# Linear attention with a swish feed-forward: kv products on two column tiles, and a reordered first chunk

## The chip, the cores and the metric

The kernel runs on one core of one Trainium2 chip. The metric is the device time of one execution in microseconds (us). A profile is one execution; its span is about 1.8 us shorter than its time in the tables.

Engines: PE is TensorE's matmul and PEld its weight load, DVE is VectorE, ACT is ScalarE, POOL is GpSimd, SP starts most DMAs.

## The reference, cut to what matters

```python
q, k, v: (8, 8, 576, 64)                       # batch, heads, tokens, head dim
q_s = softmax(q, over head dim); k_s = softmax(k, over tokens)
kv  = einsum('bhsd,bhse->bhde', k_s, v)        # one 64x64 matrix per head
x   = einsum('bhsd,bhde->bhse', q_s, kv)       # heads side by side: (4608, 512)
h   = x @ w_in                                 # (4608, 2048)
out = (h * sigmoid(beta * h)) @ w_out          # (4608, 512)
```

The two products with w_in and w_out are nearly all of the work. The kernel handles 9 chunks of 512 tokens (the first 512 tokens of each batch, and one chunk with the 64 last tokens of all batches). While chunk n runs, side work prepares the attention of a later chunk.

## The kernel before

A chunk has 16 *units* j. Unit j is one `mm_a` (h: four matmuls of 512 columns, then a tanh on ACT and a gate on DVE) and one `mm_b` (four matmuls into the output accumulators, from the gate of unit j - 2). The parts that the change touches, with cuts marked:

```python
FIX, LASTMAIN, COLT = False, True, False
...
def kv_mm(b, jj, n=2, tag="att"):              # n pairs of heads
    t = ps.tile([P, n, 2 * D1], F32, ...)      # D1 = 65: 64 columns of v, and one for the sum
    for jl in range(n):
        j = n * jj + jl
        if b < NW: ...                         # batches 0 and 1 have another layout
        if COLT: ...                           # written, but off: see the change
        for i in range(R):                     # a pair of heads at once: 128x128 by 128x130
            nc.tensor.matmul(t[:, jl, :], ek[b][:, i, 2*j:2*j+2, :]..., va[b][:, i, 2*j:2*j+2, :]..., ...)
        nc.tensor.matmul(t[:, jl, :], ekt[...][:, ds(j * P, P)], vt[...]..., ...)   # the 64 last tokens
...
pool_cast(("in", 3), ("out", 3))               # POOL casts the last block of w_in to bf16
...
for u in range(4, NJ):                         # chunk 0, units 4 to 15
    if not (FIX and u == 5):
        mm_a(0, u)
    if FIX and u == 4:
        mm_a(0, 5)
        mm_b(0, 2)
        continue
    if FIX and u in (12, 14):                  # transposes of batch 1's q on PE
        for j in (u - 12, u - 11):
            q_pet(1, j, nc.scalar if u == 12 else nc.vector)
    mm_b(0, u - LAG)                           # LAG = 2
    if u in (9, 10): q_exp(1, u - 9)           # ACT
    if u in (9, 11): q_sum(1, (u - 9) // 2)    # DVE
    if u in (10, 12): q_mul(1, (u - 10) // 2)  # DVE: the softmax multiply
    if not FIX and u in (11, 13):
        for j in (u - 11, u - 10):
            q_pet(1, j, nc.scalar if u == 11 else nc.vector)
    if u >= 12: kz_exp(1, u - 12)              # ACT: exponentials of batch 1's k
    ...
def side(n, u):                                # chunks 1 to 8
    ...
    if u in (8 + o, 10 + o) and kb < B:        # kv in two groups of two pairs
        kv_mm(kb, (u - 8 - o) // 2)
        kv_norm(kb, (u - 8 - o) // 2)
    if 11 <= u < 15:                           # x: one matmul of 512 columns per pair
        x_mm(qc, u - 11, ...)
```

The softmax here doesn't subtract the row's maximum and nothing guards it: scores larger than these inputs give would overflow.

Of the kernel before, what the change touches and what calls it, by code (L numbers as in the profile page):

```python
# [9 lines left out]
BF16 = mybir.dt.bfloat16  # L10
F32 = mybir.dt.float32
# [6 lines left out]
def kernel(  # L18
# [10 lines left out]
    nc = tc.nc  # L29
    P = nc.NUM_PARTITIONS  # L30
    B, H, S, D = q.shape
# [5 lines left out]
    HP = H // 2  # L37
    R = 4
    MAIN = R * P
    TAIL = S - MAIN  # L40
    RW = 2 * S // P
    NW = 2
    D1 = D + 1
    LAG = 2
    FIX, LASTMAIN, COLT = False, True, False
    NCH = B + 1
    order = list(range(NCH))
    if LASTMAIN:
# [6 lines left out]
    ps = ctx.enter_context(tc.tile_pool(name="ps", bufs=1, space=bass.MemoryType.PSUM))  # L55
# [7 lines left out]
    kvp = const.tile([P, B, HP, P], BF16, name="kvp")  # L63
# [5 lines left out]
    def x_of(c):  # L69
        return xT[2] if c == B else xT[c % 2]  # L70
# [6 lines left out]
    ek, eq, rq, qsT = {}, {}, {}, {}  # L77
# [63 lines left out]
    def evac(eng, dst, src):  # L141
        if eng is nc.scalar:
            eng.copy(dst, src)
        else:
            eng.tensor_copy(dst, src)  # L145
# [18 lines left out]
    def k_exp(b, s, n=2):  # L164
        if s == 0:
            ek_buf(b)
        m = H // n
        h = slice(s * m, (s + 1) * m)
        nc.scalar.activation(
            ek[b][:, :, h, :].rearrange("p i h d -> p h i d"),  # L170
            k_st[b][:, h, 0 : R * D].rearrange("p h (i d) -> p h i d", i=R),
            ACTF.Exp,
        )

    def ktail_exp(b):
        e = slice((b % 2) * TAIL, (b % 2 + 1) * TAIL)
        nc.scalar.activation(
            ekt[(b // 2) % 2][e].rearrange("p (h d) -> p h d", h=H),
            k_st[b][e, :, R * D : R * D + D],
            ACTF.Exp,  # L180
        )

    def v_buf(b):
        t = work.tile([P, HP * RW * D1], BF16, tag="va", bufs=2, name=f"va{b}")
        if b < NW:
            va[b] = t[:].rearrange("p (j i x) -> p j i x", j=HP, i=RW)
        else:
            va[b] = t[:, 0 : R * H * D1].rearrange("p (i h x) -> p i h x", i=R, h=H)
        nc.gpsimd.memset(va[b][:, :, :, D:D1], 2.0)
# [8 lines left out]
    def v_cast(b, eng):  # L198
        evac(
            eng,  # L200
            va[b][:, :, :, 0:D].rearrange("p i h d -> p h i d"),
            v_st[b][:, :, 0 : R * D].rearrange("p h (i d) -> p h i d", i=R),
        )

    def vtail_cast(b, eng):
        e = b % 2
        rr = slice(e * TAIL, (e + 1) * TAIL)
        eng.tensor_copy(vt[(b // 2) % 2][rr, e, :, 0:D], v_st[b][rr, :, R * D : R * D + D])

    def q_exp(b, s, n=2):  # L210
        if s == 0:
            eq[b] = work.tile([P, R, H, D], BF16, tag="eq", bufs=2, name=f"eq{b}")
        m = H // n
        nc.scalar.activation(  # L214
            eq[b][:, :, s * m : (s + 1) * m, :].rearrange("p i h d -> p h i d"),
            q_st[b][:, s * m : (s + 1) * m, :].rearrange("p h (i d) -> p h i d", i=R),
            ACTF.Exp,
        )

    def q_sum(b, s, n=2):  # L220
        if s == 0:
            rq[b] = work.tile([P, 2, R, H], F32, tag="rq", bufs=2, name=f"rq{b}")
        m = H // n
        h = slice(s * m, (s + 1) * m)
        nc.vector.tensor_reduce(rq[b][:, 0, :, h], eq[b][:, :, h, :], axis=AX.X, op=ALU.add)  # L225
        nc.vector.reciprocal(rq[b][:, 1, :, h], rq[b][:, 0, :, h])

    def q_mul(b, s, n=2):
        m = H // n
        h = slice(s * m, (s + 1) * m)  # L230
        nc.vector.tensor_tensor(  # L231
            eq[b][:, :, h, :],
            eq[b][:, :, h, :],
            rq[b][:, 1, :, h].unsqueeze(3).to_broadcast((P, R, m, D)),
            ALU.mult,
        )

    def q_xbar(b):
        qsT[b] = work.tile([P, R, HP, P], BF16, tag="qsT", bufs=2, name=f"qsT{b}")
        nc.sync.dma_start_transpose(  # L240
            qsT[b][:].rearrange("p i j r -> p (i j) r"),
            eq[b][:].rearrange("p i h d -> p (i h d)"),
        )
# [11 lines left out]
        evac(eng, qsT[b][:, :, j, :], t[:])  # L255

    def kv_mm(b, jj, n=2, tag="att"):
        t = ps.tile([P, n, 2 * D1], F32, tag=tag, bufs=2 if tag == "att" else 1, name=f"kv{b}_{jj}")
        att_of[b, jj] = t
        for jl in range(n):  # L260
            j = n * jj + jl
            if b < NW:
                for i in range(RW):
                    nc.tensor.matmul(
                        t[:, jl, 0:D1],
                        ek[b][:, j, i, :],
                        va[b][:, j, i, :],
                        start=(i == 0),
                        stop=(i == RW - 1),
                    )  # L270
                continue
            if COLT:
                for i in range(R + 1):
                    for e in range(2):
                        hd = 2 * j + e
                        nc.tensor.matmul(
                            t[e * D : (e + 1) * D, jl, 0:D1],
                            ek[b][:, i, hd, :] if i < R else ekt[(b // 2) % 2][:, ds(hd * D, D)],
                            va[b][:, i, hd, :] if i < R else vt[(b // 2) % 2][:, b % 2, hd, :],
                            start=(i == 0),  # L280
                            stop=(i == R),
                            tile_position=(0, e * D),
                        )
                continue
            for i in range(R):
                nc.tensor.matmul(
                    t[:, jl, :],
                    ek[b][:, i, 2 * j : 2 * j + 2, :].rearrange("p h d -> p (h d)"),
                    va[b][:, i, 2 * j : 2 * j + 2, :].rearrange("p h d -> p (h d)"),
                    start=(i == 0),  # L290
                    stop=False,
                )
            nc.tensor.matmul(
                t[:, jl, :],
                ekt[(b // 2) % 2][:, ds(j * P, P)],
                vt[(b // 2) % 2][:, b % 2, 2 * j : 2 * j + 2, :].rearrange("p h d -> p (h d)"),
                start=False,
                stop=True,
            )

    def kv_norm(b, jj, n=2):
        t = att_of.pop((b, jj))
        rk = work.tile([P, n, 1], F32, tag="rk", bufs=2, name=f"rk{b}_{jj}")
        nc.vector.reciprocal(rk[:], t[:, :, D : D + 1])
        for e in range(2):
            r = slice(e * D, (e + 1) * D)
            dst = kvp[r, b, n * jj : n * jj + n, e * D : (e + 1) * D]
            src = t[r, :, 0:D] if b < NW or COLT else t[r, :, e * D1 : e * D1 + D]
            nc.vector.tensor_tensor(dst, src, rk[r].to_broadcast((D, n, D)), ALU.mult)  # L309

    def x_mm(c, j, eng, tag="att"):
        t = ps.tile([P, MAIN], F32, tag=tag, bufs=2, name=f"x{c}_{j}")
        if c < B:
            nc.tensor.matmul(t[:], kvp[:, c, j, :], qsT[c][:, :, j, :])  # L314
        else:
            for b in range(B):
                i, e = divmod(b, 2)
                nc.tensor.matmul(
                    t[:, ds(b * TAIL, TAIL)],
                    kvp[:, b, j, :],  # L320
                    qsT[B][:, i, j, ds(e * TAIL, TAIL)],
                )
        evac(eng, x_of(c)[:, j, :], t[:])

    h_of = {}

# [261 lines left out]
    def side(n, u):  # L588
        if n + 1 >= NCH:
            return  # L590
        qc = order[n + 1]
        kb = n + 1
        o = 2 if n == 1 else 0
        if u in (2 + o, 3 + o):
            q_exp(qc, u - 2 - o)
            q_sum(qc, u - 2 - o)
        if u in (4 + o, 5 + o):
            q_mul(qc, u - 4 - o)
            if kb < B:
                k_exp(kb, u - 4 - o)  # L600
        if u == 4 + o and kb < B:
            v_buf(kb)
            v_cast(kb, nc.gpsimd)
            vtail_cast(kb, nc.gpsimd)
        if u == 6 + o:
            if kb < B:
                ktail_exp(kb)
            q_xbar(qc)
        if u in (8 + o, 10 + o) and kb < B:
            kv_mm(kb, (u - 8 - o) // 2)  # L610
            kv_norm(kb, (u - 8 - o) // 2)
        if 11 <= u < 15:
            j = u - 11
            x_mm(qc, j, nc.scalar if j % 2 == 0 else nc.vector)
        if u == 9 and n + 2 < NCH:
            load_next(n + 2)
# [3 lines left out]
    for n in range(1, NCH):  # L620
        c = order[n]
# [47 lines left out]
```

## Time and profile before

| | before |
|---|---|
| time, median of 3 runs | 291.29 us (291.06 to 291.44) |
| span of the profiled run (time 292.26 us, above these three) | 290.5 us |
| PE busy | 278.6 us, 96% |
| chunks 2 to 5, each | 29.78 to 29.79 us |
| kv of one batch on PE | 1.14 us |

From the page of the kernel before: the span, the busy times and the chain of work that ended last.

```profile
span 290.5 us, 3880 instructions
...
PE 278.6 (96%) x1447; PEld 131.0 (45%) x1475; DVE 185.2 (64%) x299; ACT 163.9 (56%) x238; POOL 41.5 (14%) x55
...
PE 87%; DMA 4%; DVE 3%; ACT 1%; issue 1%; another core or an unknown queue 1%; SPq 0%; POOL 0%; ACTq 0%
```

PE is busy for 96% of the span and makes 87% of the chain: PE bounds this kernel. The windows view cuts the run into stretches. The first row below runs from unit 6 of chunk 0 to the first x matmul of batch 1 (I call this the *late stage* of chunk 0); the second is one chunk of the steady part.

```profile
core 0: us, PE busy (x) PEld busy (x) DVE busy (x) ACT busy (x) POOL busy (x), PEclk, DMA share, GB/s
26.40:49.69 23.29, 21.63 (x140) 10.72 (x142) 16.46 (x27) 14.85 (x23) 12.24 (x14) 1.00 1.07 364
...
108.53:138.32 29.79, 29.63 (x150) 14.01 (x152) 19.55 (x32) 17.42 (x26) 3.11 (x4) 1.00 0.57 169
```

In the steady chunk PE is busy for 29.63 of 29.79 us, so whatever leaves PE there shortens the run by as much. In the late stage it is busy for 21.63 of 23.29 us. The timeline of PE shows a kv group of the kernel before (start, duration, instruction; durations overlap, so read the starts):

```profile
183.59 0.38 PE L362 MATMUL acc_3_1880<-w_out_b,g_6_1939 128*128 128x512 bf16 x1
183.81 0.39 PE L286 MATMUL kv_0_1974<-va_1913,ek_1911 128*128 128x130 bf16 x4
184.04 0.22 PE L293 MATMUL kv_0_1974<-vt_76,ekt_78 128*128 128x130 bf16 x1
184.09 0.39 PE L286 MATMUL kv_0_1974<-va_1913,ek_1911 128*128 128x130 bf16 x4
184.32 0.22 PE L293 MATMUL kv_0_1974<-vt_76,ekt_78 128*128 128x130 bf16 x1
184.38 1.03 PE L334 MATMUL h_9_1989<-xT_81,w_in_b 128*128 128x512 bf16 x4
```

From the 130-column matmul at 183.81 to the next h matmul at 184.38 is 0.57 us for 10 matmuls, 57 ns each; a batch has two such groups, 1.14 us. There is no gap before or after a group.

```profile
36.27 1.87 DVE L231 TENSOR_TENSOR eq_485<-eq_485,rq_487 128x1024 bf16<-128x1024 bf16 x1
```

```profile
36.02 1.04 POOL L145 CAST w_in_b<-w_in_114 128x1024 bf16<-128x1024 f32 x1 [2.14 <-DMA w_in_114<-in_moe_w_in_dram]
```

The transposes (`tp_0`) start at 38.29, after 1.37 us of idle that ended with DVE's softmax multiply. Unit 12 (`h_12`) follows them at 38.73.

### The profile page before, as it was taken

What the parts mean: (1) busy time and instruction counts of PE and PEld (TensorE: products, weight loads), DVE (VectorE), ACT (ScalarE), POOL (GpSimd) and SP (SyncE); (2) the same over time, 40 slices, a digit from 0 to 9 for tenths busy, and PEclk for the clock granted to TensorE, in tenths of its full rate; (3) what the DMA queues carried; (4) which work ended last, traced back from release to release, by engine and by line L of the source; (5) the groups of instructions that cost most, each with busy time, mean ns of one, the idle gap of its engine ahead of it and who ended that gap; (6) DMA issues with size and microseconds to landing.
All of it is one profiled execution on the core that took longest, in us unless ns stands there. A gap on an engine that the chain in (4) does not pass through costs nothing.

```text
span 290.5 us, 3880 instructions
## 1 busy us (share of the span) xinstructions
PE 278.6 (96%) x1447; PEld 131.0 (45%) x1475; DVE 185.2 (64%) x299; ACT 163.9 (56%) x238; POOL 41.5 (14%) x55
## 2 busy tenths in 40 slices
PE   8779979999999999999999999999999999999994
PEld 2434435445444544454445444544455444444441
DVE  7837596695678546955695469546955595454442
ACT  4853676694387347734682568355944564454341
POOL 4349670300030011001200030003000000000000
PEclk9999999999999999999999999999999999999998
DMA  7999999808941972198119902785381033005003
GB/s 248 376 384 378 377 384 316 252 0 218 315 156 38 309 197 105 47 320 217 72 78 271 272 28 118 172 226 146 144 166 53 1 147 72 0 0 147 0 0 144
DMA packets 56226, 50.06 MB, mean 172 GB/s; under 512 B 26240, under 2 KB 47760, under 8 KB 56208
## 3 DMA queue, kind: packets, MB, share of 16 engines
q1 hardware_dynamic: 56064, 49.56, 55.7%
q8 instruction: 11, 0.18, 0.3%
q10 hardware_dynamic: 144, 0.26, 0.2%
q14 instruction: 7, 0.06, 0.1%
HBM read 36.71 MB, written 9.44 MB: 159 GB/s over the span
## 4 chain that ended last, share of the span: by engine, by line
PE 87%; DMA 4%; DVE 3%; ACT 1%; issue 1%; another core or an unknown queue 1%; SPq 0%; POOL 0%; ACTq 0%
DMA k_st_86<-in_k_dram 2%; DMA w_in_97<-in_moe_w_in_dram 2%; PE acc_2_2486 L362 1%; PE acc_0_2173 L362 1%; PE acc_3_724 L362 1%; PE acc_2_2731 L362 1%; PE acc_0_2484 L362 1%; PE acc_2_2175 L362 1%; PE acc_2_1879 L362 1%; PE acc_0_1877 L362 1%; PE acc_1_1589 L362 1%; PE acc_3_2176 L362 1%; PE acc_0_1588 L362 1%; PE acc_2_1012 L362 1%; PE acc_0_1010 L362 1%; PE acc_0_721 L362 1%
## 5 line engine op out<-in xcount | busy, mean ns | idle before, releaser
L334 PEld LDWEIGHTS <-w_in_b 128*128 128x128 bf16 x576 | 55.3, 98 | 66.7 <-issue 2.7
L158 ACT ACTIVATE ek_144<-k_st_86 64x576 bf16<-64x576 f32 x8 | 5.5, 681 | 1.5 <-DVE eq_189 L231 1.4
L426 PEld LDWEIGHTS <-kvp 128*128 128x128 bf16 x34 | 3.6, 112 | 5.7 <-issue 2.8
L145 POOL CAST va_2209<-v_st_2014 128x2048 bf16<-128x2048 f32 x1 | 1.9, 1918 | 29.1 <-DMA v_st_2014<-in_v_dram 29.1
L145 POOL CAST va_1913<-v_st_1718 128x2048 bf16<-128x2048 f32 x1 | 1.9, 1920 | 28.5 <-DMA v_st_1718<-in_v_dram 28.5
L145 POOL CAST va_1624<-v_st_1429 128x2048 bf16<-128x2048 f32 x1 | 1.9, 1917 | 26.7 <-DMA v_st_1429<-in_v_dram 26.7
L158 ACT ACTIVATE ek_149<-k_st_118 64x576 bf16<-64x576 f32 x8 | 5.4, 675 | 0.0
L145 POOL CAST va_1046<-v_st_836 128x2048 bf16<-128x2048 f32 x1 | 1.9, 1919 | 24.2 <-DMA v_st_836<-in_v_dram 24.2
L145 POOL CAST va_1335<-v_st_1140 128x2048 bf16<-128x2048 f32 x1 | 1.9, 1922 | 22.3 <-DMA v_st_1140<-in_v_dram 22.3
L314 PEld LDWEIGHTS <-kvp 128*128 128x128 bf16 x32 | 3.1, 98 | 4.2 <-DVE kvp L309 1.0
L214 ACT ACTIVATE eq_189<-q_st_83 128x1024 bf16<-128x1024 f32 x2 | 2.1, 1056 | 3.0 <-DMA q_st_83<-in_q_dram 3.0
L145 POOL CAST va_147<-v_st_91 128x576 bf16<-128x576 f32 x4 | 2.7, 668 | 7.8 <-DMA v_st_91<-in_v_dram 7.6
L145 POOL CAST va_783<-v_st_132 128x2048 bf16<-128x2048 f32 x1 | 1.9, 1916 | 12.3 <-DMA v_st_132<-in_v_dram 12.3
L145 POOL CAST w_in_b<-w_in_114 128x1024 bf16<-128x1024 f32 x2 | 3.0, 1536 | 2.1 <-DMA w_in_114<-in_moe_w_in_dram 2.1
L231 DVE TENSOR_TENSOR eq_485<-eq_485,rq_487 128x1024 bf16<-128x1024 bf16 x2 | 3.1, 1542 | 0.0
L334 PE MATMUL h_0_316<-xT_80,w_in_b 128*128 128x512 bf16 x4 | 1.5, 380 | 1.5 <-POOL w_in_b L145 1.3
L145 POOL CAST w_out_b<-w_out_116 128x1024 bf16<-128x1024 f32 x2 | 2.6, 1298 | 1.7 <-DMA w_out_116<-in_moe_w_out_dram 1.7
L145 DVE CAST w_in_b<-w_in_102 128x1024 bf16<-128x1024 f32 x2 | 2.6, 1312 | 0.0
L225 DVE TENSOR_REDUCE rq_748<-eq_746 128x16 f32<-128x1024 bf16 x2 | 2.4, 1214 | 0.3 <-ACT eq_746 L214 0.3
L225 DVE TENSOR_REDUCE rq_487<-eq_485 128x16 f32<-128x1024 bf16 x2 | 2.4, 1213 | 0.3 <-ACT eq_485 L214 0.3
L225 DVE TENSOR_REDUCE rq_191<-eq_189 128x16 f32<-128x1024 bf16 x2 | 2.4, 1215 | 0.2 <-ACT eq_189 L214 0.2
L145 POOL CAST w_out_b<-w_out_100 128x1024 bf16<-128x1024 f32 x2 | 2.1, 1040 | 3.3 <-DMA w_out_100<-in_moe_w_out_dram 3.3
(1460 smaller groups left out, 839.6 us busy)
## 6 DMA issues: line engine op xcount, KB each, us to landing
k_st_86<-in_k_dram SPq DMA_DIRECT2D x4, 288.0 KB, 7.0
v_st_91<-in_v_dram SPq DMA_DIRECT2D x4, 288.0 KB, 7.8
k_st_118<-in_k_dram SPq DMA_DIRECT2D x4, 288.0 KB, 9.7
v_st_124<-in_v_dram SPq DMA_DIRECT2D x2, 576.0 KB, 9.3
q_st_83<-in_q_dram SPq DMA_DIRECT2D x2, 512.0 KB, 4.3
w_in_97<-in_moe_w_in_dram SPq DMA_DIRECT2D x2, 512.0 KB, 6.4
w_out_100<-in_moe_w_out_dram SPq DMA_DIRECT2D x2, 512.0 KB, 8.6
w_in_102<-in_moe_w_in_dram SPq DMA_DIRECT2D x1, 1024.0 KB, 9.3
```

Of the source, the lines that this page charges most:

```text
L145: eng.tensor_copy(dst, src)
L158: nc.scalar.activation(ek[b][r, j : j + m, :, e * D : (e + 1) * D], k_st[b][r, j : j + m, :].rearrange("p j (i d) -> p j i d", i=RW), ACTF ...
L214: nc.scalar.activation(eq[b][:, :, s * m : (s + 1) * m, :].rearrange("p i h d -> p h i d"), q_st[b][:, s * m : (s + 1) * m, :].rearrange(" ...
L225: nc.vector.tensor_reduce(rq[b][:, 0, :, h], eq[b][:, :, h, :], axis=AX.X, op=ALU.add)
L231: nc.vector.tensor_tensor(eq[b][:, :, h, :], eq[b][:, :, h, :], rq[b][:, 1, :, h].unsqueeze(3).to_broadcast((P, R, m, D)), ALU.mult,)
L314: nc.tensor.matmul(t[:], kvp[:, c, j, :], qsT[c][:, :, j, :])
L334: nc.tensor.matmul(h[:], w_in_b[:, kt, ds(j * P, P)], x_of(c)[:, kt, :], start=(kt == 0), stop=(kt == KT - 1),)
L362: nc.tensor.matmul(acc[st][:], g[:, ds(st * P, P)], w_out_b[:, j, :], start=(j == 0), stop=(j == NJ - 1),)
L426: nc.tensor.matmul(t[:, 0:cols], kvp[:, B - 1, 0, :], kvp[:, B - 1, :, :].rearrange("p j r -> p (j r)")[:, 0:cols],)
```

## The change

The intent: the kv products of batches 2 to 7 run on two 128x64 column tiles of the array, so that two heads' matmuls of 65 columns stream side by side in place of one of 130 columns, in one group of 40 matmuls per batch; and in chunk 0 the transposes of batch 1 come one unit later, so that unit 12's matmuls fill the wait for DVE, with unit 5 led ahead of unit 2's second product.

```diff
-    FIX, LASTMAIN, COLT = False, True, False
+    FIX, LASTMAIN, COLT, XT4 = True, True, True, False
...
-        t = ps.tile([P, n, 2 * D1], F32, ...)
+        t = ps.tile([P, n, D1 if b < NW or COLT else 2 * D1], F32, ...)
...
+    def x_tiles(c): ...      # x on four 64x64 tiles: only used if XT4
+    def x_evac(c, jh): ...
...
-        if u in (8 + o, 10 + o) and kb < B:
-            kv_mm(kb, (u - 8 - o) // 2)
-            kv_norm(kb, (u - 8 - o) // 2)
-        if 11 <= u < 15:
+        if u == 9 + o // 2 and kb < B:
+            kv_mm(kb, 0, n=HP)
+            kv_norm(kb, 0, n=HP)
+        if XT4 and u == 12 and qc < B:
+            x_tiles(qc)
+        if XT4 and u in (12, 13) and qc < B:
+            x_evac(qc, u - 12)
+        if (qc == B or not XT4) and 11 <= u < 15:
```

With `COLT` on, this code, which the kernel before already holds, runs:

```python
for i in range(R + 1):                   # 4 blocks of 128 tokens, and the 64 last
    for e in range(2):                   # the two heads of a pair, on two tiles
        hd = 2 * j + e
        nc.tensor.matmul(t[e*D:(e+1)*D, jl, 0:D1],
                         ek[b][:, i, hd, :] if i < R else ekt[...][:, ds(hd * D, D)],
                         va[b][:, i, hd, :] if i < R else vt[...][:, b % 2, hd, :],
                         ..., tile_position=(0, e * D))
```

(`FIX` also guards the queue of an output store, in a branch that does not run here, so it acts in chunk 0 alone.)

More of the change, by code (lines that the diff above doesn't have):

```diff
@@ L257, in kv_mm @@
     def kv_mm(b, jj, n=2, tag="att"):
-        t = ps.tile([P, n, 2 * D1], F32, tag=tag, bufs=2 if tag == "att" else 1, name=f"kv{b}_{jj}")
+        t = ps.tile([P, n, D1 if b < NW or COLT else 2 * D1], F32, tag=tag, bufs=2 if tag == "att" else 1, name=f"kv{b}_{jj}")
         att_of[b, jj] = t
@@ L323, in x_mm, with x_tiles, x_evac @@
         evac(eng, x_of(c)[:, j, :], t[:])
+    xp_of = {}
+    def x_tiles(c):
+        xp_of[c] = [ps.tile([P, HP, MAIN // 2], BF16, tag="att", bufs=2, name=f"xp{c}_{e}") for e in range(2)]
+        for j in range(HP):
+            for th in range(2):
+                for e in range(2):
+                    r = slice(e * D, (e + 1) * D)
+                    nc.tensor.matmul(
+                        xp_of[c][e][th * D : (th + 1) * D, j, :],
+                        kvp[r, c, j, e * D : (e + 1) * D],
+                        qsT[c][r, 2 * th : 2 * th + 2, j, :],
+                        tile_position=(e * D, th * D),
+                    )
+    def x_evac(c, jh):
+        for e in range(2):
+            for th in range(2):
+                evac(
+                    nc.scalar if th == 0 else nc.vector,
+                    x_of(c)[e * D : (e + 1) * D, 2 * jh : 2 * jh + 2, th * 256 : th * 256 + 256],
+                    xp_of[c][e][th * D : (th + 1) * D, 2 * jh : 2 * jh + 2, :],
+                )
     h_of = {}
```

## The prediction

> **What bounds the kernel now.** TensorE. The page shows PE busy 278.6 of 290.5 us, and the chain of waits is 87% PE. In the busy times by stretch, each middle chunk takes 29.7 to 29.8 us with PE busy for 29.6 of it. The timeline there is gap-free, 0.215 us per 512-column matmul. ACT (56%), DVE (64%) and DMA are not limiting in chunks 1 to 8. PE's waits outside the head and the tail are one group in chunk 0: the batch-1 transposes wait 1.4 us for DVE's softmax multiply, and about 0.5 us more goes idle round the second pair.
>
> **What the change touches, per batch 2 to 7 (six times).**
> - kv: 20 matmuls of 130 columns, 57 ns each, 1.14 us. After: 40 of 65 columns on two column tiles.
> - x (changed too, though the short description omits it): 4 matmuls of 512 columns, 0.86 us. After: 16 of 256 columns on four 64x64 tiles.
>
> If tiles overlapped perfectly and nothing else cost time, kv would take 20 x 32 ns = 0.64 us (32 ns is the pace of the 65-column matmuls of batches 0 and 1: 18 in 0.58 us) and x 4 x 110 ns = 0.44 us. That would save 0.92 us per batch, 5.5 us in all.
>
> Against it: the Trainium skill, "TensorEngine Tiling (Array Packing)", Key Properties and Restrictions, says that a change of tiling mode drains TensorE and that column tiling disables Fast Weight Load. Four mode changes per batch are added. The only one that this trace can show is the 16-row transpose of beta: the two changes round it take about 0.27 us more than its columns need, so about 0.14 us each. Four make an estimated 0.4 to 0.55 us per batch, most of the ideal gain. Weight loads double for kv and quadruple for x, and may not hide behind 65 columns. I estimate kv at 0.75 to 1.1 us, x at 0.45 to 0.6 us, and 0.4 us of drain: between 0.1 us lost and 0.4 us won per batch; centre 0.15, so 0.9 us in six.
>
> **Chunk 0.** The transposes move behind one more h unit (0.86 us of matmuls that are ready), so of the 1.4 us wait about 0.6 remains; the second pair's wait shrinks as well. ACT's exponentials of batch 1 end just before kv needs them. Gain about 1.0 us, all on the chain. The swap of units saves nothing: PE has no gap there.
>
> **Off the chain.** x gets 8 evictions of 64 partitions in place of 4 of 128 (ACT +1.2 us per batch at 0.58 us each), in units 12 and 13; kv_norm costs DVE about 0.5 us less. Both engines have 1 us idle per unit there, so I expect no new PE wait.
>
> **Prediction.** 289.4 us, 0.65% faster; 8 in 10 between 287.0 and 292.0. Faster by over 2%: 0.06; within 2%: 0.89; slower by over 2%: 0.05.
>
> **What would show it.** Transposes' wait on DVE falls from 1.4 to about 0.6 us. Chunks 2 to 6 shrink from 29.7 by 0 to 0.4 us. Gaps of about 0.1 us stand before and after each kv and x group. The 40-matmul kv group spans 0.75 to 1.1 us from first start to the next full-array start.
>
> **What would make it wrong.** Weight loads of the tiles run one after another at over 50 ns: kv takes 2 us, and the total is 4 to 6 us longer. Mode changes cost nothing: 4 us or more is saved, nearing 285. Evictions of x delay a tanh so far that PE waits for h. A rearranged chunk 0 makes PE wait for ACT's exponentials, losing the 1.0 us again.

## More of the kernel before

The longest wait of PE in the late stage of chunk 0 is this one, shown here with the instructions of DVE and POOL that matter for it:

```profile
36.54 0.38 PE L362 MATMUL acc_3_380<-w_out_b,g_9_479 128*128 128x512 bf16 x1
38.29 0.38 PE L250 MATMUL tp_0_521<-identity,eq_485 128*128 128x128 bf16 x4 [1.37 <-DVE eq_485 L231]
...
38.73 1.03 PE L334 MATMUL h_12_533<-xT_80,w_in_b 128*128 128x512 bf16 x4
```

## The result, and the profile after

| | before | after |
|---|---|---|
| first measurement: median of 6 runs each | 291.27 us | 290.51 us (290.21 to 290.93) |
| ratio, with 95% interval | | 0.9971 (0.9953 to 0.999) |
| second measurement, another chip job: medians (11 and 6 runs) | 291.53 us | 290.04 us (289.29 to 290.47) |
| ratio, with 95% interval | | 0.9943 (0.9924 to 0.9962) |
| span of the profiled run | 290.5 us | 289.1 us |
| chunks 2 to 5, each | 29.78 to 29.79 us | 29.51 us |
| late stage of chunk 0 | 23.29 us | 23.65 us |

A ratio is the mean time of one kernel's runs over the mean of the other's runs of the same rounds, so it is not quite the ratio of the medians. Executions over 1.5% slower than the fastest of the same kernel are left out of the means. The two measurements of the same two kernels differ by 0.28% of the time, 0.8 us: single runs of one kernel scatter by as much, and in the profiles it is the start of the run that moves (unit 6 of chunk 0 begins at 26.30 us in one profile of after and at 25.86 us in another, after_again; from there to the end they take 262.80 and 262.82 us). Both agree that the change is a small gain, 0.8 us or 1.7 us by their ratios; the forecast was 1.9 us. For the parts of the change, the lengths of stages within the profiles are the sharper measure: the chunks repeat to 0.01 us.

The same lines of the page of the kernel after:

```profile
span 289.1 us, 4130 instructions
...
PE 279.2 (97%) x1595; PEld 127.9 (44%) x1595; DVE 181.9 (63%) x281; ACT 163.7 (57%) x238; POOL 41.0 (14%) x55
...
PE 83%; DMA 6%; DVE 5%; ACT 2%; SPq 1%; issue 1%; ACTq 0%
```

The same two stretches in the windows view:

```profile
core 0: us, PE busy (x) PEld busy (x) DVE busy (x) ACT busy (x) POOL busy (x), PEclk, DMA share, GB/s
26.30:49.95 23.65, 21.96 (x142) 10.64 (x142) 15.53 (x27) 14.71 (x22) 11.95 (x15) 1.00 1.07 366
...
108.25:137.76 29.51, 29.51 (x174) 13.54 (x172) 19.08 (x29) 17.41 (x26) 1.40 (x3) 1.00 0.57 170
```

PE's share of the chain fell from 87% to 83%, with more of DMA and DVE in it. The steady chunk is 0.28 us shorter, and PE's busy time now fills it. (That time counts the modelled ends of matmuls, and so covers the gaps of 0.1 us that are read off below.) The late stage of chunk 0 is 0.36 us longer. The kv group of the kernel after in the timeline of PE:

```profile
184.48 0.38 PE L386 MATMUL acc_3_1940<-w_out_b,g_7_2015 128*128 128x512 bf16 x1
184.79 0.32 PE L276 MATMUL kv_0_2047<-va_1973,ek_1971 128*64 128x65 bf16 x8
184.94 0.20 PE L276 MATMUL kv_0_2047<-vt_76,ekt_78 128*64 128x65 bf16 x2
184.97 0.29 PE L276 MATMUL kv_0_2047<-va_1973,ek_1971 128*64 128x65 bf16 x8
...
185.28 0.30 PE L276 MATMUL kv_0_2047<-va_1973,ek_1971 128*64 128x65 bf16 x8
185.41 0.20 PE L276 MATMUL kv_0_2047<-vt_76,ekt_78 128*64 128x65 bf16 x2
185.55 1.04 PE L358 MATMUL h_10_2107<-xT_81,w_in_b 128*128 128x512 bf16 x4
```

The first matmuls of successive pairs of heads, 10 matmuls each, start 0.15 to 0.18 us apart, against 0.28 us before; the group starts at 184.79 and the next h matmul at 185.55, 0.76 us for 40 matmuls. The matmul before the group started at 184.48 and takes 0.215 us of streaming, as its neighbours do, so PE was free at about 184.69: there is a gap of 0.10 us before the group. The last two matmuls start at 185.41 and stream for about 0.03 us, so there is a gap of 0.11 us after it too. The whole costs 0.10 + 0.65 + 0.11 = 0.86 us in place of 1.14.

In chunk 0 the wait is still there, but its owner has changed:

```profile
36.44 0.38 PE L386 MATMUL acc_3_380<-w_out_b,g_9_479 128*128 128x512 bf16 x1
38.34 1.04 PE L358 MATMUL h_12_520<-xT_80,w_in_b 128*128 128x512 bf16 x4 [1.52 <-POOL w_in_b L145]
39.21 0.39 PE L250 MATMUL tp_0_530<-identity,eq_485 128*128 128x128 bf16 x4
```

```profile
36.17 1.21 DVE L231 TENSOR_TENSOR eq_485<-eq_485,rq_487 128x1024 bf16<-128x1024 bf16 x1
```

```profile
36.65 1.63 POOL L145 CAST w_in_b<-w_in_114 128x1024 bf16<-128x1024 f32 x1 [2.11 <-DMA w_in_114<-in_moe_w_in_dram]
```

```profile
PE h_12_520 L358 <- POOL w_in_b L145: 1.5, 1, 1.5
PE h_6_433 L358 <- DVE g_4_414 L370: 0.5, 1, 0.5
```

Unit 12 now waits 1.52 us for POOL's cast of `w_in_b`; the first half of that cast, which holds the columns of units 12 and 13, started at 36.65 and took 1.63 us. The transposes behind it wait for nothing. DVE's multiply, which took 1.87 us in the profile of before, took 1.21 us here. The x matmuls are as before, one of 512 columns per pair of heads:

```profile
189.01 0.38 PE L314 MATMUL x_0_2133<-qsT_2006,kvp 128*128 128x512 bf16 x1
```

### The profile page after: what moved, and what is told of

The parts are those of the page before. It is cut to its first block, busy times and chain, and to the rows that moved or that the text cites. A ratio compares the mean times of both kernels' runs of the same rounds, so it can differ in the third digit from the quotient of the medians.

```text
span 289.1 us, 4130 instructions
## 1 busy us (share of the span) xinstructions
PE 279.2 (97%) x1595; PEld 127.9 (44%) x1595; DVE 181.9 (63%) x281; ACT 163.7 (57%) x238; POOL 41.0 (14%) x55
## 4 chain that ended last, share of the span: by engine, by line
PE 83%; DMA 6%; DVE 5%; ACT 2%; SPq 1%; issue 1%; ACTq 0%
DMA w_in_102<-in_moe_w_in_dram 4%; DMA v_st_91<-in_v_dram 2%; PE acc_3_2822 L386 1%; PE acc_3_1636 L386 1%; PE acc_1_1026 L386 1%; PE acc_1_2820 L386 1%; PE acc_3_2577 L386 1%; PE acc_0_2248 L386 1%; PE acc_3_1940 L386 1%; PE acc_1_1938 L386 1%; PE acc_0_721 L386 1%; PE acc_1_2575 L386 1%; PE acc_0_2574 L386 1%; PE acc_2_2250 L386 1%; PE acc_1_1634 L386 1%; PE acc_3_1332 L386 1%
## 5 line engine op out<-in xcount | busy, mean ns | idle before, releaser
L145 POOL CAST w_out_b<-w_out_100 128x1024 bf16<-128x1024 f32 x2 | 2.1, 1040 | 4.8 <-DMA w_out_100<-in_moe_w_out_dram 4.8
L225 DVE TENSOR_REDUCE rq_191<-eq_189 128x16 f32<-128x1024 bf16 x2 | 2.4, 1215 | 0.3 <-ACT eq_189 L214 0.3
L225 DVE TENSOR_REDUCE rq_487<-eq_485 128x16 f32<-128x1024 bf16 x2 | 2.4, 1216 | 0.3 <-ACT eq_485 L214 0.3
L225 DVE TENSOR_REDUCE rq_748<-eq_746 128x16 f32<-128x1024 bf16 x2 | 2.4, 1212 | 0.3 <-ACT eq_746 L214 0.3
L225 DVE TENSOR_REDUCE rq_1947<-eq_1945 128x16 f32<-128x1024 bf16 x2 | 2.4, 1192 | 0.3 <-ACT eq_1945 L214 0.3
L225 DVE TENSOR_REDUCE rq_2584<-eq_2582 128x16 f32<-128x1024 bf16 x2 | 2.4, 1191 | 0.3 <-ACT eq_2582 L214 0.3
L225 DVE TENSOR_REDUCE rq_1035<-eq_1033 128x16 f32<-128x1024 bf16 x2 | 2.4, 1191 | 0.3 <-ACT eq_1033 L214 0.3
```

The costliest lines, as they stand in the source:

```text
L145: eng.tensor_copy(dst, src)
L225: nc.vector.tensor_reduce(rq[b][:, 0, :, h], eq[b][:, :, h, :], axis=AX.X, op=ALU.add)
```

## The experiments

All kernels below are built from the kernel after by its own flags and the edits shown. The table collects the chunk 0 measurements: the late stage (first matmul of unit 6 to first x matmul of batch 1, from the timeline), and the time. The kernel before of the same rounds is the base of each ratio.

| kernel | kv on tiles | order in chunk 0 | late stage, us | median, us | ratio (95%) |
|---|---|---|---|---|---|
| before | no | before | 23.29 | see above | 1 |
| after | yes | change | 23.65 | 290.51 | 0.9971 (0.9953 to 0.999) |
| after_again | yes | change | 23.66 | 290.04 | 0.9943 (0.9924 to 0.9962) |
| colt_only | yes | before | 23.02 | 290.25 | 0.9964 (0.9933 to 0.9995) |
| fix_only | no | change | 23.66 | 291.93 | 1.0013 (0.9993 to 1.0032) |
| lead_only | no | only the lead of unit 5 | 23.01 | 291.77 | 1.0002 (0.9983 to 1.0021) |
| before_free | no | before, unit 12 free | 22.64 | 291.62 | 0.9997 (0.9974 to 1.002) |
| fix_free | no | change, unit 12 free | 21.96 | 290.91 | 0.9968 (0.9945 to 0.9991) |
| b10_first | yes | unit 10 ahead | 22.70 | 289.94 | 0.9958 (0.9924 to 0.9991) |
| b10_kz | yes | and exponentials earlier | 24.50 | 291.24 | 0.9988 (0.9968 to 1.0008) |
| b10_kz_dve | yes | and copies on DVE | 23.66 | 290.51 | 0.9963 (0.9945 to 0.9981) |
| fix_cast | yes | change, cast on ACT | 22.99 | 289.53 | 0.9923 (0.9905 to 0.994) |
| b10_cast | yes | unit 10 ahead, cast on ACT | 22.32 | 289.74 | 0.9929 (0.9907 to 0.995) |

My theory after the first look: the kv part gives 0.275 us in each of six chunks, 1.65 us, and the chunk 0 part gives nothing or costs something, because unit 12 is not ready. The rival: the kv part gives less, and chunk 0 is neutral or gains.

### The two parts alone

```diff
# colt_only
-    FIX, LASTMAIN, COLT, XT4 = True, True, True, False
+    FIX, LASTMAIN, COLT, XT4 = False, True, True, False
# fix_only: FIX on, COLT off, and the kv groups of before (two, at units 8 and 10)
```

> Only the kv part of the change (128x64 column tiles, one group of 40, for batches 2 to 7); chunk 0 is as before. My theory: all of the gain is here, 0.275 us in each of six chunks, so 1.65 us less than before: 289.6 us, ratio 0.994, and chunks of 29.51 instead of 29.78 us. Rival (the kv gain is partly lost elsewhere and chunk 0 is neutral): no better than the whole change, 290.5 us.

> Only the chunk 0 part (transposes of batch 1 one unit later, unit 5 leads); kv as before. My theory: no gain, 0 to 0.9 us slower than before (291.3 to 292.2 us), because the unit put ahead of the transposes waits for GpSimd's cast of the last w_in block (about 1.5 us of wait). The step of my prediction (rival): 1.0 us faster, 290.3 us.

```profile
36.83 0.61 PE L250 MATMUL tp<-identity,eq 128*128 128x128 bf16 x8 [0.71 <-DVE eq L231]
37.63 1.04 PE L358 MATMUL h<-xT,w_in_b 128*128 128x512 bf16 x4 [0.20 <-POOL w_in_b L145]
```

These two lines are of colt_only; the next is unit 12 of fix_only:

```profile
37.82 1.04 PE L358 MATMUL h<-xT,w_in_b 128*128 128x512 bf16 x4 [1.52 <-POOL w_in_b L145]
```

In colt_only the steady chunk took 29.51 us, as expected (x matmuls of successive chunks at 99.13 and 128.64). Its ratio, 0.9964, is a smaller gain than the 0.994 that I expected, and its interval holds both; one of its six runs was 292.69 us, at a slightly lower granted clock (0.992). In fix_only the late stage took 23.66 us, just that of the whole change, unit 12 waited 1.5 us for POOL, and the time did not fall: ratio 1.0013. So the gain of the change is that of the kv part, and the predicted 1.0 us of chunk 0 is not there. A measure that leaves out the unsteady start says so more sharply: from the start of unit 6 to the end of the profile, lead_only (below; the kernel before but for a neutral lead) takes 263.75 us, colt_only 1.58 us less, fix_only 0.68 us more, and the kernel after, with both parts, 0.95 us less (the one profile of before takes 264.07 us). These are single profiles, but the two of the kernel after differ by only 0.02 us.

```diff
# lead_only: COLT and FIX off, and
-        if not (FIX and u == 5):
+        if u != 5:
             mm_a(0, u)
-        if FIX and u == 4:
+        if u == 4:
```

> Only the lead of unit 5 in chunk 0; everything else as before. My theory: neutral within 0.2 us in the stage from unit 6 on, since unit 6 waits for VectorE's cast of w_in block 1 and the gate behind it with either order; the loss of the chunk 0 part is in the transposes alone. Rival: the lead is what costs 0.5 us, seen as a wait of unit 6 for VectorE's gate of unit 4 and a later start of unit 6 relative to the end of that cast than in the kernel before.

The late stage took 23.01 us (kv in the groups of before), the same as 23.02 in colt_only, which has no lead. Unit 6 did wait 0.68 us for the gate of unit 4, but it started 0.64 us after DVE's cast of w_in block 1 had ended (26.38 after 25.74), and in b10_first, which has no lead, 0.65 us after (25.33 after 24.68). The lead is neutral; it only moves a wait from unit 5 to unit 6. (The stage of 23.29 us in the profile of before is longer than these two because of DVE's stretched multiply; see below.)

### Is it unit 12's weights?

Two kernels with a wrong result, both with COLT off and the kv groups of before; FIX is off in before_free and on in fix_free. Units 12 to 15 of chunk 0 use the w_in columns of units 8 to 11. All loads and casts stay.

```diff
-                w_in_b[:, kt, ds(j * P, P)],
+                w_in_b[:, kt, ds((j - 4 if c == 0 and j >= 12 else j) * P, P)],
```

> Wrong result on purpose: in chunk 0 units 12 to 15 use the w_in columns of units 8 to 11, so they don't wait for the last w_in block; all loads and casts are kept; otherwise the kernel before. Control of the next run. My theory: same as before within 0.3 us, as TensorE waits there for VectorE's multiply ahead of the transposes, and unit 12 comes after them.

> Wrong result on purpose: the same substitution, with the chunk 0 part of the change on and kv as before. My theory: with the wait for the last w_in block taken away the predicted gain comes back, 0.8 to 1.1 us less than before_free (about 290.3 us), the transposes waiting about 0.6 us for VectorE. Rival (the chain of ScalarE's exponentials of batch 1 bounds the end of chunk 0 anyway, or the lead of unit 5 costs time): less than 0.4 us gained.

With the weights no longer waited for, the order of the change takes 0.68 us less in the late stage than the order of before (21.96 against 22.64); with the real weights it takes 0.64 us more (23.66 against 23.01 or 23.02). The 0.68 us is a little under the 0.8 to 1.1 us that I had expected. The times point the same way, though their intervals overlap: the mean of six runs is 290.67 us for fix_free and 291.53 us for before_free. In fix_free unit 12 follows unit 9's product without a gap, and the transposes follow unit 12 without one:

```profile
36.77 1.03 PE L358 MATMUL h<-xT,w_in_b 128*128 128x512 bf16 x4
37.64 0.61 PE L250 MATMUL tp<-identity,eq 128*128 128x128 bf16 x8
```

So the idea of the change was right and its premise wrong: the work put into the gap was not ready. I had expected the transposes still to wait 0.6 us for DVE; in this run the multiply was done in time.

### Why POOL's cast is late: two instructions that take turns

Over the traces, DVE's multiply and POOL's first half cast overlap in time, and one of the two is always stretched. A cast of this size takes 1.04 us alone and the multiply 1.21 us. In the profile of before the cast came first (36.02 to 37.06) and the multiply took 1.87 us, ending 1.08 us after the cast. In the other fourteen profiles the multiply came first; it took 1.21 us, and the cast took 1.63 to 2.04 us, the longer the more of it lay beside the multiply, and ended 0.89 to 0.90 us after the multiply in each. (fix_free shows the other order once more: its second multiply began during POOL's cast of w_out, took 1.46 us and ended 1.07 us after the cast.) The Trainium skill, "SBUF — State Buffer", section "SBUF: two separate sides", says that a DVE instruction with two SBUF inputs and a GpSimd one that reads SBUF share a port pair as an exclusive lock: the one that starts first holds it for the whole instruction, and "the other fully blocks". These traces agree: all but about 0.14 us of the second one's work came after the end of the first.

This explains why exchanging the transposes and unit 12 on PE could not win: the transposes need the multiply and unit 12 needs the cast, the two take turns on one port, and neither order makes both ready before 2.1 us after the first of them started. It also tells that the 1.4 us on which I built the forecast was one outcome of a race, and the rare one, seen in 1 of 15 profiles: in colt_only, lead_only and before_free, with the same order of transposes, they waited 0.7 us in this place.

If this is so, the cast should move to an engine that does not use that port. ACT idles there.

```diff
# fix_cast: the kernel after, and
-    pool_cast(("in", 3), ("out", 3))
+    w_cast("in", 3, 1, nc.gpsimd)
+    pool_cast(("out", 3))
...
+        if u == 11:
+            w_cast("in", 3, 0, nc.scalar)
```

> The kernel after the change, with one thing moved: the first half of the last w_in block (the half that units 12 and 13 need) is cast by ScalarE, which idles there, at the same time as GpSimd casts the second half. My theory: unit 12 waits 0.4 to 0.6 us instead of 1.5 us, and the stage from unit 6 to the x matmuls of batch 1 takes 22.4 to 22.8 us instead of 23.65; about 0.9 us less time than the kernel after. Rival (something else than that cast makes the change's order slow): still 23.4 us or more.

```profile
35.29 1.21 DVE L231 TENSOR_TENSOR eq<-eq,rq 128x1024 bf16<-128x1024 bf16 x1
...
35.66 1.73 POOL L145 CAST w_in_b<-w_in 128x1024 bf16<-128x1024 f32 x1 [2.14 <-DMA w_in<-in_moe_w_in_dram]
35.69 1.03 ACT L143 CAST w_in_b<-w_in 128x1024 bf16<-128x1024 f32 x1
...
36.78 0.82 PE L358 MATMUL h<-xT,w_in_b 128*128 128x512 bf16 x3 [0.85 <-ACT w_in_b L143]
```

The two halves start together, at 35.66 on POOL and 35.69 on ACT, while DVE's multiply runs (35.29 to 36.50). ACT needs 1.03 us, POOL 1.73: the half on ACT is not stretched beside the multiply. Unit 12 starts at 36.78 after 0.85 us of wait (I had expected 0.4 to 0.6), and the late stage takes 22.99 us (expected 22.4 to 22.8): 0.66 us less than the kernel after, with a right result. The theory held in kind, less in size: 22.99 us is just the 23.02 us of colt_only, so moving the cast took back what the reordering had cost and won no more. With the weights free the same order took 21.96 us.

### Work that is ready

```diff
# b10_first: COLT on, FIX off, and
+        if u == 12:                       # unit 10's second product first
+            mm_b(0, 10)
+            for j in (0, 1):
+                q_pet(1, j, nc.scalar)
         mm_a(0, u)
+        if u == 14:
+            for j in (2, 3):
+                q_pet(1, j, nc.vector)
-        mm_b(0, u - LAG)
+        if u != 12:
+            mm_b(0, u - LAG)
...                                       (the old transposes at u = 11 and 13 are removed)
# b10_cast: this, and the edit of fix_cast
# b10_kz: this, and
-        if u >= 12:
-            kz_exp(1, u - 12)
+        if 11 <= u < 15:
+            kz_exp(1, u - 11)
# b10_kz_dve: b10_kz with q_pet(1, 0..1) evicted by DVE and q_pet(1, 2..3) moved behind mm_b(0, 13)
```

> kv part on; chunk 0: the transposes of batch 1 wait behind the second product of unit 10 (whose inputs are ready) instead of behind unit 12 (whose weights are not), no lead of unit 5. My theory: the work put ahead must be work that is ready; the 0.86 us of unit 10 now lies in the wait, so unit 12 starts when its weights are cast and everything after it is up to 0.86 us earlier, unless ScalarE's chain of copies, tanhs and exponentials of batch 1 bounds the end of chunk 0, which I estimate to leave 0.2 to 0.5 us. Time 0.2 to 0.8 us below the kernel with the kv part alone, about 289.7 us. Rival (any reordering of the transposes costs, as in the change): 290.3 us or more.

The late stage took 22.70 us, 0.32 us below colt_only and 0.95 us below the kernel after. The second product of unit 10 has its inputs by then, so it fills the gap. In time the gain over colt_only is inside the scatter (289.94 against 290.25 us, in different jobs; each has one run above 292 us, at a granted clock of 0.992 or 0.993).

> b10_first with the same move of the cast. My theory: unit 12 no longer waits for GpSimd, but ScalarE's chain of copies, tanhs and exponentials of batch 1 already bounds the end of chunk 0, so only 0.1 to 0.5 us are gained on b10_first's stage of 22.70 us: 22.2 to 22.6 us.

22.32 us, within the expected band.

> As b10_first, and ScalarE's exponentials of batch 1's k are issued one unit earlier (from unit 11 on, ahead of unit 12's tanh). My theory: after b10_first the end of chunk 0 is bounded by ScalarE's chain of copies, tanhs and exponentials; started about 1 us earlier, it ends about 1 us earlier, so from unit 6 to the x matmuls of batch 1 it takes 22.70 - 0.6 to 1.0 us, and the time is 0.5 to 0.9 us below b10_first's 289.9 us. Rival (the late tanhs then hold up TensorE, or k of batch 1 has not landed by then): no gain or a loss.

> As b10_kz, with the first pair's copies on VectorE instead of ScalarE (1.07 us less on ScalarE's chain) and the second pair of transposes one unit later. My theory: a further 0 to 0.5 us on the stage from unit 6 to x, if ScalarE still bounds it. Rival: VectorE's later gates make it 0 to 0.5 us worse than b10_kz.

A miss. The stage grew to 24.50 us, and the rival was right:

```profile
37.66 1.37 ACT L158 ACTIVATE ek<-k_st 64x576 bf16<-64x576 f32 x2 [1.93 <-DMA k_st<-in_k_dram]
```

```profile
PE tp L250 <- DVE eq L231: 2.6, 2, 1.7
PE h L358 <- DVE g L370: 1.5, 1, 1.5
```

Moved ahead, the exponential waited on ACT 1.93 us for k of batch 1 to land; the copies and the tanh of unit 12 ran only after it (at 39.06 and 40.16 us), and PE waited 1.5 us for the gate. With the copies on DVE and the second transposes later (two edits, not told apart) it was 23.66 us: 0.84 us below b10_kz, more than the 0 to 0.5 us expected, but still 0.96 us above b10_first. The end of chunk 0 is hemmed in by loads as well: the windows view gives the DMA engines a busy share of 1.07 over the late stage in both kernels.

> The kernel after the change, unaltered, timed on the same chip as the two above: ratio to before 0.997 as measured at first, 0.5 to 1.5 us slower than the two above if they are an improvement; its stage from unit 6 to x should again be 23.6 us, with a 1.5 us wait for GpSimd's cast.

The stage was 23.66 us and unit 12's wait 1.5 us, as expected. The ratio, 0.9943, was a larger gain than at first. Measured beside b10_kz and b10_kz_dve, the kernel after has the lowest ratio of the three (its interval is clear of that of b10_kz and overlaps that of b10_kz_dve), so those two are no improvement on it.

### What makes the kv part worth 0.28 us

```diff
# colt_two: colt_only with the kv groups of before
-        if u == 9 + o // 2 and kb < B:
-            kv_mm(kb, 0, n=HP)
-            kv_norm(kb, 0, n=HP)
+        if u in (8 + o, 10 + o) and kb < B:
+            kv_mm(kb, (u - 8 - o) // 2)
+            kv_norm(kb, (u - 8 - o) // 2)
# colt_serial: colt_only with the loops over e and i exchanged
-                for i in range(R + 1):
-                    for e in range(2):
+                for e in range(2):
+                    for i in range(R + 1):
```

> kv part on, but in two groups of 20 matmuls two units apart, as before, instead of one of 40; chunk 0 as before. My theory (each change of tiling mode costs about 0.12 us, and there are two more per batch): a chunk takes 0.24 us more than with one group, 29.75 instead of 29.51 us, nearly the 29.78 of before. Rival (the gaps before and after the group are waits for ScalarE's tanh, which the profile names there, or come once per batch): 29.51 to 29.6 us.

Successive chunks are 29.74 us apart (x matmuls at 99.27 and 129.01), against 29.51 us with one group: 0.23 us for two more changes of tiling mode per batch. The median was 291.24 us, the ratio 0.9989 (0.9965 to 1.0013). Almost all of the gain was given back, so putting all heads in one group is what makes the tiles pay. This also answers the rival: the wait view names ACT's tanh as what ended the idle time before a group, but a gap of about 0.1 us comes before each group, at whichever unit it stands (three of the twelve read 0.2 us more, where one of the four matmuls ahead has no record), and in the kernel before, with full-array groups at the same units, there is none. The Trainium skill, "TensorEngine Tiling (Array Packing)", Key Properties, says that a change of mode drains the engine. The traces agree and give a size: 0.10 us going in and 0.11 us coming out in the timeline, 0.115 us on average by colt_two.

> kv part on in one group of 40, but each head's five matmuls follow one another on the same column tile, instead of alternating between the two tiles; chunk 0 as before. My theory (the gain comes from two matmuls of 65 columns streaming side by side, 31 ns per pair): without alternation about 29 ns each, 1.2 us plus 0.24 us of mode changes, so chunks of 30.1 us. Rival (the gain comes from halving the columns of each weight load and output, whatever the order): unchanged, 29.51 us.

My theory fell here. Successive chunks are 29.57 us apart (x at 99.41 and 128.98), only 0.06 us more than with alternation, not 0.6 us (median 290.55 us, ratio 0.9963, 0.9941 to 0.9984). From the start of the group in the timeline of PE:

```profile
95.13 0.34 PE L276 MATMUL kv<-va,ek 128*64 128x65 bf16 x7
95.28 0.20 PE L276 MATMUL kv<-vt,ekt 128*64 128x65 bf16 x1
95.31 0.20 PE L276 MATMUL kv<-va,ek 128*64 128x65 bf16 x2
95.34 0.20 PE L276 MATMUL kv<-vt,ekt 128*64 128x65 bf16 x1
```

In the program the first head's matmul with `vt`, `ekt` is the fifth of the group, behind four with `va`, `ek`, and the next head's five follow on the other tile. The program as built still has them in this order. In the trace it starts eighth, in this group and in the five others, with seven ahead of it: three of the second head's matmuls had started before the first head's last. So PE does not need them to alternate in the program; here it started later matmuls on the other tile ahead of an earlier one. The group then takes 0.82 us (95.13 to the next h matmul at 95.95) instead of 0.76. As both orders overlap, this run does not separate my theory from its rival; the pace does. At the 0.215 us per 512 columns of the h matmuls, 65 columns are an estimated 27 ns, and 40 such matmuls one after another 1.1 us; the 40 on two tiles took 0.65 us. They ran side by side.

## Why the prediction was right or wrong

**What bounds the kernel: right.** PE. The 0.275 us that left PE per chunk left the chunk.

**That x changes too: wrong, a misreading.** The prediction says that the code changes x to 16 matmuls on 64x64 tiles. The flag `XT4` that guards it is `False`, and the profile after shows the 512-column x matmuls and no extra evictions. What I wrote on x and on its evictions was about code that does not run. (With the flag on, the kernel does not even build: its tiles take bf16 where a matmul's output must be fp32.)

**kv: mechanism right, size too small.** Overlap of the two tiles and drains at mode changes are both there. I put the mode change at 0.14 us from one small transpose; it is 0.10 to 0.12. I put the group at 0.75 to 1.1 us, and drains on top. The matmuls measured 0.65 us, 32 ns per pair, which is the ideal pace, with no sign of a slower weight load. (By the check that the prediction names, from the first start to the next full-array start, the group takes 0.76 us, at the edge of its 0.75 to 1.1.) The forecast for kv and x together was 0.15 us per batch, 0.9 us in six; kv alone gave 0.275 and 1.65. The mis-sized terms are the time of the tiled matmuls (0.65 us for the 40, not 0.75 or more) and two drains too many. By the prediction's own terms kv with its two drains would have won between -0.16 and 0.19 us, about nothing, and nearly all of the 0.15 us came from x, which did not change: that 0.9 us is of the right order is luck.

**Chunk 0: wrong, and this is the step that failed.** The prediction says that the transposes move behind "one more h unit (0.86 us of matmuls that are ready), so of the 1.4 us wait about 0.6 remains", for 1.0 us. The matmuls are not ready. Unit 12 is the first that reads the last w_in block, whose cast on POOL takes turns with the very multiply that the transposes wait for. The runs showed: a wait of 1.5 us in the same place with another owner, a late stage 0.64 us longer than with the same kernel without it (23.65 to 23.66 against 23.01 to 23.02; 0.36 us longer than in the one profile of before), a gain of 0.68 us when unit 12 is freed of those weights, and the loss undone, but no gain, when half of the cast moves to ACT (0.66 us off the kernel after, level with colt_only). In the profile before, this wait was hidden: PE reached unit 12 only after the transposes, when its weights were done (in colt_only, where the transposes came sooner, a wait of 0.2 us for POOL is left there). And the 1.4 us itself was the longer of two outcomes of a race.

**The lead of unit 5: right.** Neutral, in lead_only.

**No new wait of PE: wrong.** Two came: unit 12 on POOL (1.5 us) and unit 6 on a gate (0.5 us). The second cost nothing.

Summed: forecast 0.9 + 1.0 = 1.9 us. Shown by stages: 1.65 us from kv, less 0.36 us (profile against profile) to 0.64 us (against the kernels whose multiply was not stretched) in chunk 0, which leaves 1.0 to 1.3 us; measured 0.8 us and 1.7 us by the two ratios. That the 1.7 us comes near the forecast is luck too: kv gave more than forecast and chunk 0 took away where it should have given. The start of the run differs by over 1 us between profiles (unit 6 of chunk 0 starts at 25.28 to 26.41 us, in 13 of the 15 profiles 0.64 to 0.76 us after the end of DVE's cast of w_in block 1); between the two profiles of the kernel after it is all of the 0.4 us by which they differ. What moves that cast, and why in several jobs the runs of one kernel fall into two clusters about 1 us apart, was not settled.

**A better version.** fix_cast has the lowest ratio, 0.9923 (0.9905 to 0.994), and its interval lies wholly below that of the kernel after in the first measurement and overlaps it in the second; b10_cast has the shortest late stage (22.32 us) and ratio 0.9929 (0.9907 to 0.995). Both are right, and by stage both beat the kernel after, by 0.66 us and 1.33 us; which of the two is faster in time is not told apart.

## What to carry to other kernels

Before moving work into a gap, list everything that the moved work waits for, also what its present place hides: in the profile before, unit 12 showed no wait on its weights only because something else made it late. When two waits end close together, ask whether their producers share something, here a port, for then exchanging the consumers gains nothing; moving one producer to another engine, or putting work that is ready ahead of both, can. Column tiles pay for small matmuls when they are batched so that the two mode changes are paid once, and a switch in a diff is read for its value before its code is costed.

## What the Trainium skill lacked or had wrong

- "TensorE: Matmul & The Clock Gate", Part 3, "What overlaps and what doesn't", says that matmuls are "pc-monotone in start AND end — strict FIFO, no reordering". In colt_serial the fifth matmul of each kv group starts eighth, behind three later ones on the other column tile, and the group of 40 takes 0.82 us, where 40 in turn at the 32 ns of the full-array 65-column matmuls would take 1.28 us.
- "TensorEngine Tiling (Array Packing)", Key Properties, has the drain at a mode change but no cost. Here: 0.10 us before and 0.11 us after a group, 0.115 us per change from two more of them per chunk (29.74 against 29.51 us).
- The same page, Restrictions, says that column tiling disables Fast Weight Load, and gives no size, which made me fear slow loads. A 128x64 load is recorded with 112 ns, a 128x128 one with 98 ns, but the matmuls keep 32 ns per pair: no cost was seen here at 65 columns, weights changed for each.
- "SBUF — State Buffer" has the shared port right; beyond two bare slowdown factors it gives no measured case of two compute instructions. Here: a 1.04 us GpSimd cast took 1.63 to 2.04 us beside a DVE multiply that started first, and a 1.21 us multiply took 1.87 us beside a cast that started first.
